# Score tiles from three 64-row products on two row groups instead of two stacked 128-row products

## The chip, the cores and the metric

The kernel runs on one core of a Trainium2 chip. Its engines are TensorE (PE in the profile; PEld is its weight load), VectorE (DVE), ScalarE (ACT), GpSimd (POOL) and SyncE (SP), which here only issues DMAs. The metric is the device time of one launch in microseconds (us): the median of the runs.

## The reference

For 8 batches with 8 heads of 576 rows and 64 columns, attention keeps the 32 largest scores of each row. Then each of the 4608 tokens goes to one of 8 experts with two layers.

```python
scores = scale * np.matmul(q, k.transpose(0, 1, 3, 2))
kth = np.partition(scores, -top_k, axis=-1)[..., -top_k:-top_k + 1]
scores = np.where(scores >= kth, scores, -1000000000.0)
attn = np.exp(scores - np.max(scores, axis=-1, keepdims=True))
attn = attn / (np.sum(attn, axis=-1, keepdims=True) + 1e-09)
x = np.matmul(attn, v)                  # per head; then [4608, 512]
logits = x @ w_gate + modality_bias[modality_id]
e_idx = np.argmax(logits, axis=1)       # gate_w: its softmax weight
h = np.maximum(x[mask] @ w1[e], 0.0)    # for each expert e
out[mask] = gate_w[mask, None] * (h @ w2[e])
```

## The kernel before, in words

Heads are worked in pairs: 32 pairs, each with nine tiles of 128 rows by 576 columns. Tiles 0 to 7 of a pair are four blocks of 128 rows for each of the two heads; the ninth holds the last 64 rows of both. A loop over steps i (L1056) records the work of all engines by hand, as a pipeline: at step i the scores of tile i + 2 are made, tile i is searched for its largest values on DVE, tile i - 9 is transposed, and the stages between run on ACT, POOL and DVE.

A score needs more precision than one pass of the fast type (fp32r) gives. So q and k are transposed on PE (prep, L280) and split into a high part and a remainder (split, L268), which lie in the tile st: two heads on partitions 0 to 63 and 64 to 127. Ten DMAs on SP's queue a pair (stack, L309) then copy them into stacked tiles. qs holds the high part of q on partitions 0 to 63 and the remainder on 64 to 127; ks holds the high part of k, or its remainder, on both halves. One product over 128 rows thus gives two terms, and two products all four. qk (L358) makes a tile in two halves of 288 columns, in two banks of PSUM, with two products each. For the ninth tile, fill (L322) copies the last 64 rows of q into two zeroed tiles qbd, one per head, and eight products of 512 or 64 columns make the tile. sevac (L375) copies a score tile from PSUM to SBUF on ACT; there is one PSUM buffer S for it.

The first pair takes no stacked tiles: unstacked (L341) makes two tiles at once, one per head, in S and T, from 64-row products out of st, four terms each.

The experts' work is cut into slots of 256 tokens. Once enough tokens are routed, a slot's matmuls (L775, L787) are recorded between the tiles. A planner decides how many: at each step it has a budget of STEP = 3.39, takes off what COST says the step's other PE work costs, and spends the rest (L1165 to L1178); where no slot is ready it records keep-warm matmuls (L913). The slots that are left at the end run alone, with products of three terms (L1005, L1021). avs and av (L491) multiply the attention weights with v, on two column groups.

Of the kernel before, what the change touches and what calls it, by code (L numbers as in the profile page):

```python
# [9 lines left out]
FT = mybir.dt.float32  # L10
# [43 lines left out]
COST = {"trans": 0.5, "qk": 0.5, "mix": 1.02, "rest": 0.22, "t": 0.11, "prep": 0.43, "logits": 1.2, "xrow": 0.54, "av": 0.49, "av8": 0.17}  # L54
# [18 lines left out]
def kernel(  # L73
# [40 lines left out]

    LD, PR, T = {}, {}, {}
# [57 lines left out]
    qbd = [[o.tile([128, 128], FR, name=f"qbd{i}{j}", bufs=1) for j in range(2)] for i, o in enumerate((const, wk))]  # L173
    for a in qbd:
        for t in a:
            V.memset(t.bitcast(FT), 0.0)
# [103 lines left out]
    def prep(p, part, first=False):  # L280
# [3 lines left out]
        if first:  # L284
            d.setdefault("st", st0)
        elif "st" not in d:
            d["st"] = wk.tile([128, 2, 2, S], FR, name="st", bufs=1)
# [16 lines left out]
        if part == "k":  # L304
            d["ks"] = wk.tile([128, 2, 2, S], FR, name="ks", bufs=2)
        else:
            d["qs"] = wk.tile([128, 2, S], FR, name="qs", bufs=2)

        def stack(h, queues=(SP, SP)):  # L309
            for v in range(2):  # L310
                if part == "k":
                    for a, b, o in ((0, S, 0),) if h == 0 else ((0, 512, 64), (512, S, -512)):
                        queues[v].dma_start(d["ks"][half(v), :, h, a + o:b + o].bitcast(FT), st[half(h), :, a:b].bitcast(FT))
                else:
                    queues[v].dma_start(d["qs"][half(v), h, :].bitcast(FT), st[half(h), v, :].bitcast(FT))

        for h in range(2):
            f = lambda h=h, **o: stack(h, **o)
# [14 lines left out]
    st0 = wk.tile([128, 2, 2, S], FR, name="ks", bufs=2)  # L333
    bd0 = wk.tile([128, 2, S], FR, name="qs", bufs=2)[:, 0, :256].rearrange("p (x s) -> p x s", x=2)

    def fill_first():
        for h in range(2):
            r = slice(h * 64, h * 64 + 64)
            G.tensor_scalar(bd0[r, :, r], PR[0]["st"][r, :, 1, 512:].bitcast(FT), 1.0, 1.0, op0=OP.mult, op1=OP.mult)

    def unstacked(j):  # L341

        if j % 2:
            return
        ps = [psS.tile([128, 2, 512], FT, name="S"), psT.tile([128, 2, 512], FT, name="T")][:1 + (j < 8)]
        for h, t in enumerate(ps):
            T[j + h] = {"ps": t[:, :, :288]}
        st = PR[0]["st"]
        r = [slice(h * 64, h * 64 + 64) if j < 8 else slice(0, 128) for h in range(2)]
        for x in range(2):  # L350
            for y in range(2):
                for h, a, b, o in ((0, 0, 288, 0), (1, 0, 64, 512), (1, 64, 288, -64), (0, 288, S, 0), (1, 288, S, -64)):
                    if h < len(ps):
                        l = bd0[:, x, :] if j == 8 else st[r[h], x, 1, j * 64:j * 64 + 128]
                        PE.matmul(ps[h][:, a // 288, a % 288:a % 288 + b - a], l, st[r[h], y, 0, a + o:b + o],
                                  start=(x + y == 0 and a % 288 == 0), stop=(x + y == 2), skip_group_check=True)

    def qk(i, p, j, bd):  # L358
        d = PR[p]
        ps = psS.tile([128, 2, 512], FT, name="S")  # L360
        for hf in range(2):
            a, b = (hf * 288, hf * 288 + 288) if j < 8 else ((0, 512), (512, S))[hf]
            if j < 8:
                c, h = divmod(j, 2)
                terms = [(d["qs"][:, h, c * 128:(c + 1) * 128], x, h, a, b, 0) for x in range(2)]
            else:
# [6 lines left out]
        T[i] = {"ps": ps[:, :, :288] if j < 8 else ps.rearrange("p a b -> p (a b)")[:, :S]}  # L373

    def sevac(i):  # L375
        T[i]["S"] = sb = wk.tile([128, S], FT, name="Ssb", bufs=LR + 1 + QL - QO)
        ps = T[i]["ps"]
        A.activation(sb.rearrange("p (a b) -> p a b", a=2) if len(ps.shape) == 3 else sb, ps, AF.Copy, scale=0.125)  # L378
# [536 lines left out]
    V.memset(bd0.bitcast(FT), 0.0)  # L915
# [21 lines left out]
    fill_first()  # L937
# [466 lines left out]
```

## Time and profile before

| | |
|---|---|
| median of 3 runs | 1266.87 us (1263.65 to 1268.3) |
| the profiled execution's own time | 1262.36 us |
| its span, first to last instruction | 1260.6 us |
| PE busy | 1181.1 us (94%) |
| PE's weight loads busy | 927.0 us (74%) |
| DVE busy | 1140.2 us (90%) |
| ACT busy | 989.0 us (78%) |
| POOL busy | 677.8 us (54%) |
| mean granted clock of PE | 0.986 |

Busy time is the union of the instructions' times on an engine. Matmuls overlap in the array, so that a matmul lasts longer than the distance to the next one: for throughput one reads the distances of starts. The granted clock is a share of 2.4 GHz: 1.00 is 2.4 GHz, 0.50 is 1.2 GHz.

### The profile page before, as it was taken

The numbers are of one execution on the slowest core, as the hardware profiler recorded it, in microseconds if no ns is written. First come the engines' busy times: TensorE is split into PE (matmuls) and PEld (weight loads), VectorE is DVE, ScalarE is ACT, GpSimd is POOL, SyncE is SP. The second block draws the span as 40 slices with busy tenths as digits, with TensorE's granted clock in tenths as the row PEclk, the third lists the DMA queues.
The fourth block names the chain that finished last, engine by engine and source line by source line (L and its number), as shares of the span: only waits on it lengthen the run. The fifth ranks groups of instructions, "written<-read, shape, count | busy, mean of one in ns | idle before, by whom it ended". The sixth has DMA issues, their size and how long they took to land. (4 is left out here: it accounts for less than half of the span.)

```text
span 1260.6 us, 28788 instructions
## 1 busy us (share of the span) xinstructions
PE 1181.1 (94%) x8032; PEld 927.0 (74%) x8032; DVE 1140.2 (90%) x5917; ACT 989.0 (78%) x2014; POOL 677.8 (54%) x1253
## 2 busy tenths in 40 slices
PE   7889987899988999989999999999999999999985
PEld 5667766768766868677777778787778775699885
DVE  6999999999999999999999999999999996477751
ACT  4999988889888988888898888888888885256542
POOL 4888865564574557554755466556755573211110
PEclk7999999999999999999999999999999999999998
DMA  4563337754356745655666566656576425478550
GB/s 107 156 186 86 87 86 224 199 150 126 86 136 188 217 117 157 189 156 139 171 184 177 146 182 191 185 154 169 161 207 178 128 71 168 150 251 275 190 174 15
DMA packets 204339, 199.28 MB, mean 158 GB/s; under 512 B 104413, under 2 KB 151533, under 8 KB 204160
## 3 DMA queue, kind: packets, MB, share of 16 engines
q1 hardware_dynamic: 196880, 177.96, 51.2%
q0 software_dynamic: 6080, 19.00, 4.2%
q8 instruction: 69, 1.13, 0.4%
q14 instruction: 110, 0.90, 0.2%
q10 hardware_dynamic: 1200, 0.30, 0.1%
HBM read 118.63 MB, written 24.23 MB: 113 GB/s over the span
## 5 line engine op out<-in xcount | busy, mean ns | idle before, releaser
L385 DVE MAX8 cand<-Ssb 128x8 f32<-128x82 f32 (+1 forms) x2016 | 429.5, 230 | 5.4 <-ACT Ssb L378 5.4
L423 POOL TENSOR_TENSOR y<-Ssb,K 128x576 f32<-128x576 f32 x288 | 370.4, 1286 | 5.7 <-ACT K L417 5.4
L417 ACT ACTIVATE K<-Ssb,n 128x576 bf16<-128x576 f32 x288 | 227.2, 789 | 29.0 <-POOL y L423 28.2
L378 ACT ACTIVATE Ssb<-S 128x576 f32<-128x576 f32 x284 | 185.9, 655 | 80.9 <-PE S L371 45.5
L371 PE MATMUL S<-ks,qs 128*128 128x288 f32 x992 | 220.3, 344 | 29.2 <-ACT Ssb L378 16.8
L427 DVE MAX8 mg<-y 128x8 f32<-128x576 f32 x288 | 214.7, 745 | 10.2 <-POOL y L423 10.2
L371 PEld LDWEIGHTS S<-ks,qs 128*128 128x128 f32 x992 | 151.5, 190 | 73.0 <-ACT Ssb L378 27.3
L775 PE MATMUL E<-xgT,w1b 128*128 128x256 f32 x816 | 196.8, 384 | 8.8 <-ACT hT L779 7.6
L441 ACT ACTIVATE ex<-Ssb,sm 128x576 f32<-128x576 f32 x256 | 199.9, 781 | 0.0
L489 ACT ACTIVATE PT<-T 128x640 f32<-128x640 f32 (+1 forms) x288 | 191.0, 663 | 5.6 <-PE T L481 5.6
L787 PE MATMUL E<-w2b,hT 128*128 128x512 f32 x400 | 188.2, 597 | 1.5 <-ACT hT L779 0.9
L447 DVE SCALAR_TENSOR_TENSOR P<-Ssb,kth,ex 128x576 f32<-128x576 f32 x224 | 188.0, 840 | 0.7 <-DVE cand L385 0.3
L481 PE MATMUL T<-idf,P 128*128 128x128 f32 x1152 | 170.4, 275 | 8.9 <-ACT P L466 8.9
L775 PEld LDWEIGHTS E<-xgT,w1b 128*128 128x128 f32 x816 | 147.5, 190 | 32.8 <-ACT hT L779 11.3
L470 POOL TENSOR_SCALAR spare<-P 1x1 f32<-1x1 f32 x224 | 50.0, 223 | 202.3 <-DVE mg L396 189.2
L481 PEld LDWEIGHTS T<-idf,P 128*128 128x128 f32 x1152 | 135.0, 140 | 17.9 <-ACT P L466 13.5
L509 PE MATMUL X<-PT,vm 128*64 128x256 f32 (+1 forms) x1536 | 145.0, 331 | 1.5 <-ACT xT L512 0.9
L410 POOL TENSOR_SCALAR n<-mg 128x1 f32<-128x1 f32 x288 | 72.8, 253 | 111.5 <-DVE mg L398 103.2
L509 PEld LDWEIGHTS X<-PT,vm 128*64 128x64 f32 x1536 | 88.4, 137 | 47.2 <-issue 10.2
L787 PEld LDWEIGHTS E<-w2b,hT 128*128 128x128 f32 x400 | 69.8, 190 | 59.7 <-issue 53.9
L1027 POOL DMA_INDIRECT out_dram<-ot,tk x12 | 12.0, 1000 | 106.7 <-ACT ot L1026 106.7
L396 DVE MAX8 mg<-cand 128x8 f32<-128x56 f32 x288 | 60.9, 211 | 0.2
(233 smaller groups left out, 2245.1 us busy)
## 6 DMA issues: line engine op xcount, KB each, us to landing
w1b<-in_moe_w_dram SPq DMA_DIRECT2D x76, 512.0 KB, 5.4
w2b<-in_moe_w_dram SPq DMA_DIRECT2D x76, 512.0 KB, 5.3
ks<-st SPq DMA_DIRECT2D x62, 288.0 KB, 3.4
qs<-st SPq DMA_DIRECT2D x124, 144.0 KB, 2.7
ks<-st SPq DMA_DIRECT2D x62, 256.0 KB, 4.8
xg<-xs SPq DMA_DIRECT2D x19, 516.0 KB, 5.1
km<-in_k_dram SPq DMA_DIRECT2D x64, 128.0 KB, 3.4
vm<-in_v_dram SPq DMA_DIRECT2D x32, 256.0 KB, 3.4
```

Source lines behind the costliest of these rows:

```text
L371: PE.matmul(ps[:, hf, u - a:v - a], l, d["ks"][:, x, h, u + o:v + o], start=(n == 0), stop=(n == len(terms) - 1), skip_group_check=(j == 8))
L385: return [lambda s=s: V.max(c[:, s * 8:s * 8 + 8], T[i]["S"][:, bnd[s]:bnd[s + 1]]) for s in range(NSUB)]
L417: A.activation(t["K"], t["S"], AF.Sign, scale=2.0 ** -24 - 1.0, bias=t["n"][:, 1, i % 3:i % 3 + 1], accum_out=t["n"][:, 0, i % 3:i % 3 + 1])
L423: G.tensor_tensor(t["y"], t["S"], t["K"], op=OP.mult)
L427: V.max(t["mg"][:, i % 3, 24:32], t["y"])
L441: A.activation(t["ex"], t["S"], AF.Exp, bias=t["s"][:, i % 3:i % 3 + 1])
L447: V.scalar_tensor_tensor(t["P"], t["S"], kth[:, i:i + 1], t["ex"], op0=OP.is_ge, op1=OP.mult, accum_out=dn)
L481: PE.transpose(T[i]["pt"][:, x, :], (Pm if c == 4 else Pb[c % 2])[:, h * 512 + x * 128:h * 512 + x * 128 + 128], idf)
L489: A.activation(o, T[i]["pt"][:, :n], AF.Copy)
L509: PE.matmul(o.rearrange("p (a b) -> p a b", a=2) if j < 8 else o, l, r, start=(c == 0), stop=(c == 4))
L775: PE.matmul(ps[:, f % 2], w1b[:, c, f * 128:(f + 1) * 128], xgT[:, c, :], start=(c == 0), stop=(c == KC - 1))
L787: PE.matmul(o["py"], hT[:, f, t * 128:(t + 1) * 128], w2b[:, f, :], start=(f == 0), stop=(f == FC - 1))
```

## The change

qk now makes each of tiles 0 to 7 from three terms (high by high, high by remainder, remainder by high) in two halves of 288 columns. A product has 64 rows. The half with g = 0 takes its operands from partitions 0 to 63, the other from 64 to 127; for the head that lies on the right partitions they come from st itself, for the other half from sw, into which cross copies each head's q and part of its k onto the other head's partitions: five DMAs a pair. st has two buffers now. The ninth tile takes six products of 128 rows and 288 columns from one zeroed tile that holds both heads' rows on its diagonal. The first pair drops the fourth term. The planner's costs of a score tile go from 0.5 to 0.4 and, for the ninth, from 1.02 to 0.8.

```diff
-COST = {"trans": 0.5, "qk": 0.5, "mix": 1.02, ...
+COST = {"trans": 0.5, "qk": 0.4, "mix": 0.8, ...
+    TERMS = ((0, 0), (0, 1), (1, 0))
-            d["st"] = wk.tile([128, 2, 2, S], FR, name="st", bufs=1)
+            d["st"] = wk.tile([128, 2, 2, S], FR, name="st", bufs=2)
...
+            d["sw"] = wk.tile([128, 2, 512 + 288], FR, name="sw", bufs=2)
+        def cross(h):
+            if part == "q":
+                cols = ((0, 512, 0),)
+            else:
+                cols = ((288, S, 512),) if h == 0 else ((512, S, 512), (0, 224, 576))
+            for a, b, o in cols:
+                SP.dma_start(d["sw"][half(1 - h), :, o:o + b - a].bitcast(FT), st[half(h), :, a:b].bitcast(FT))
...
     def fill(p, bd):
         for h in range(2):
-            G.tensor_scalar(bd[h][:, h * 64:h * 64 + 64], PR[p]["qs"][:, h, 512:].bitcast(FT), 1.0, 1.0,
-                            op0=OP.mult, op1=OP.mult)
+            r = slice(h * 64, h * 64 + 64)
+            G.tensor_scalar(bd[r, :, r], PR[p]["st"][r, :, 1, 512:].bitcast(FT), 1.0, 1.0, op0=OP.mult, op1=OP.mult)
...
     def unstacked(j):
-        for x in range(2):
-            for y in range(2):
+        for x, y in TERMS:
...
     def qk(i, p, j, bd):
-        for hf in range(2):
-            a, b = (hf * 288, hf * 288 + 288) if j < 8 else ((0, 512), (512, S))[hf]
-            if j < 8:
-                c, h = divmod(j, 2)
-                terms = [(d["qs"][:, h, c * 128:(c + 1) * 128], x, h, a, b, 0) for x in range(2)]
-            else:
-                terms = [(bd[0], x, 0, a, b, 0) for x in range(2)]
-                for u, v, o in ((a, min(b, 512), 64), (512, b, -512)):
-                    terms += [(bd[1], x, 1, u, v, o) for x in range(2)] if u < v else []
-            for n, (l, x, h, u, v, o) in enumerate(terms):
-                PE.matmul(ps[:, hf, u - a:v - a], l, d["ks"][:, x, h, u + o:v + o], start=(n == 0),
-                          stop=(n == len(terms) - 1), skip_group_check=(j == 8))
+        c, h = divmod(j, 2)
+        for x, y in TERMS:
+            for g in range(2):
+                r = slice(g * 64, g * 64 + 64)
+                if j == 8:
+                    l, m = bd[:, x, :], st[:, y, 0, g * 288:g * 288 + 288]
+                elif g == h:
+                    l, m = st[r, x, 1, c * 128:c * 128 + 128], st[r, y, 0, h * 224:h * 224 + 288]
+                else:
+                    l, m = d["sw"][r, x, c * 128:c * 128 + 128], d["sw"][r, y, 512:]
+                PE.matmul(ps[:, g, :288], l, m, start=(x + y == 0), stop=(x == 1), skip_group_check=True)
```

On PE, at a ninth tile and the tile behind it, in the stage in which expert work runs between the tiles, the program before has these rows (S is the score tile, T the transposes' tile, E the experts'; P and idf are transposed values and the identity):

```order
L775 MATMUL E<-xgT,w1b 128x256 x4
L371 MATMUL S<-ks,qbd_117 128x512 x2
L371 MATMUL S<-ks,qbd_118 128x512 x2
L371 MATMUL S<-ks,qbd_117 128x64 x2
L371 MATMUL S<-ks,qbd_118 128x64 x2
L481 MATMUL T<-idf,P_124 128x128 x4
L775 MATMUL E<-xgT,w1b 128x256 x6
L371 MATMUL S<-ks,qs 128x288 x4
L481 MATMUL T<-idf,P_124 128x128 x5
```

On PE in the changed program, at such a place, L762 and L774 are the experts' lines, L360 is qk's and L468 the transposes':

```order
L762 MATMUL E<-xgT,w1b 128x256 x6
L360 MATMUL S<-st,qbd_116 128x288 x6
L468 MATMUL T<-idf,P_120 128x128 x4
L774 MATMUL E<-w2b,hT 128x512 x3
L360 MATMUL S<-st 128x288
L360 MATMUL S<-sw 128x288
L360 MATMUL S<-st 128x288
L360 MATMUL S<-sw 128x288
L360 MATMUL S<-st 128x288
L360 MATMUL S<-sw 128x288
L468 MATMUL T<-idf,P_120 128x128 x5
```

The ninth tile has six equal products where it had eight of two widths. An ordinary tile has six products that alternate between st and sw, and so between the two halves of the partitions, where it had four; expert matmuls still stand ahead of it and transposes behind it.

On SP's queue, the copies of one pair before:

```order
L313 DMA ks<-st 64x2x576 x2
L313 DMA ks<-st 64x2x512
L313 DMA ks<-st 64x2x64
L313 DMA ks<-st 64x2x512
L313 DMA ks<-st 64x2x64
L315 DMA qs<-st 64x576 x4
```

The copies of one pair on SP's queue in the changed program:

```order
L312 DMA sw<-st 64x2x288
L312 DMA sw<-st 64x2x64
L312 DMA sw<-st 64x2x224
L312 DMA sw<-st 64x2x512 x2
```

Ten transfers became five, at the same places of the queue.

## Rows read from the trace of the kernel before

**Rows 1.** Busy time by stretch: start:end, length, each engine's busy (instructions), PEclk, DMA.

```profile
8.00:25.00 17.00, 15.62 (x88) 12.75 (x86) 11.88 (x81) 7.17 (x15) 9.21 (x19) 0.50 0.33 80
40.00:280.00 240.00, 210.74 (x1640) 165.86 (x1638) 237.99 (x1324) 214.37 (x468) 170.31 (x266) 1.00 0.55 146
280.00:560.00 280.00, 264.94 (x1833) 205.73 (x1831) 274.30 (x1505) 240.61 (x496) 159.96 (x305) 0.99 0.55 152
560.00:1040.00 480.00, 473.08 (x3153) 364.89 (x3151) 469.30 (x2552) 413.21 (x850) 289.69 (x553) 1.00 0.60 164
1080.00:1230.00 150.00, 145.99 (x897) 126.86 (x896) 97.69 (x262) 75.91 (x117) 21.05 (x48) 1.00 0.64 215
```

**Rows 2.** Waits, 560 to 1040 us: engine line <- releaser: us in total, times, longest.

```profile
ACT Ssb L378 <- PE S L371: 27.0, 29, 1.8
```

**Rows 3.** Timeline of PE, 700 to 708 us: start, length of the group, instructions.

```profile
699.62 1.67 PE L775 MATMUL E<-xgT,w1b 128*128 128x256 f32 x7
700.95 1.64 PE L371 MATMUL S<-ks,qbd 128*128 128x512 f32 x8
702.42 0.65 PE L481 MATMUL T<-idf,P 128*128 128x128 f32 x4
702.91 2.76 PE L775 MATMUL E<-xgT,w1b 128*128 128x256 f32 x12
705.32 0.88 PE L371 MATMUL S<-ks,qs 128*128 128x288 f32 x4
706.03 0.71 PE L481 MATMUL T<-idf,P 128*128 128x128 f32 x5
```

**Rows 4.** Timeline of PE in the startup, 12.7 to 13.2 us.

```profile
12.78 0.44 PE L355 MATMUL S<-ks 64*128 64x288 f32 x1
12.79 0.53 PE L355 MATMUL T<-ks 64*128 64x224 f32 x1
13.02 0.44 PE L355 MATMUL S<-ks 64*128 64x288 f32 x1
13.12 0.47 PE L355 MATMUL T<-ks 64*128 64x288 f32 x1
```

**Rows 5.** Timeline of PE around products on two column groups, 314.3 to 318.4 us.

```profile
314.35 0.27 PE L290 MATMUL X<-idf,kqt 128*128 128x128 f32 x1
314.55 1.95 PE L509 MATMUL X<-PT,vm 128*64 128x256 f32 x16
...
316.76 0.63 PE L509 MATMUL X<-PT,vm 128*64 128x64 f32 x16
317.22 0.29 PE L509 MATMUL X<-PT,vt 128*64 128x64 f32 x4
317.44 0.80 PE L371 MATMUL S<-ks,qs 128*128 128x288 f32 x4
318.08 0.49 PE L481 MATMUL T<-idf,P 128*128 128x128 f32 x3
```

**Rows 6.** Timeline of PE and its loads at the first pair; [idle before <- releaser].

```profile
14.85 0.18 PEld L290 LDWEIGHTS X<-idf,kqt 128*128 128x128 f32 x1 [0.25 <-issue]
...
21.52 1.05 PE L297 MATMUL X<-idf,qm 128*128 128x128 f32 x4
22.51 0.28 PEld L355 LDWEIGHTS S<-ks 64*128 64x128 f32 x1 [0.33 <-issue]
...
22.51 0.61 PE L355 MATMUL S<-ks 64*128 64x288 f32 x1
22.92 0.44 PE L355 MATMUL S<-ks 64*128 64x288 f32 x1
```

**Rows 7.** Waits, 40 to 1040 us.

```profile
PE S L371 <- DMA qs<-st: 8.3, 5, 2.9
```

**Rows 8.** All instructions of L371: count, ns min/median/max, first and last start.

```profile
L371 PE MATMUL S<-ks,qs x992: 289/296/702, 31.9 to 1030.0; 128*128 128x288 f32 x199
L371 PE MATMUL S<-ks,qbd x248: 191/332/802, 54.2 to 1033.7; 128*128 128x512 f32 x62, 128*128 128x64 f32 x62
```

More of the change, by code (lines that the diff above doesn't have):

```diff
@@ L53 @@
 AV7 = (0, 5)
-COST = {"trans": 0.5, "qk": 0.5, "mix": 1.02, "rest": 0.22, "t": 0.11, "prep": 0.43, "logits": 1.2, "xrow": 0.54, "av": 0.49, "av8": 0.17}
+COST = {"trans": 0.5, "qk": 0.4, "mix": 0.8, "rest": 0.22, "t": 0.11, "prep": 0.43, "logits": 1.2, "xrow": 0.54, "av": 0.49, "av8": 0.17}
 RN = 6
@@ L171 @@
     G.iota(tokc[:, 4:5], pattern=[[1, 1]], base=512, channel_multiplier=1, allow_small_or_imprecise_dtypes=True)
[L173 to L176, printed above, removed]
+    qbd = [o.tile([128, 2, 128], FR, name=f"qbd{i}", bufs=1) for i, o in enumerate((const, wk))]
+    for t in qbd:
+        V.memset(t.bitcast(FT), 0.0)
     Pb = [wk.tile([128, 2 * S], FT, name=f"P{i}", bufs=1) for i in range(2)]
@@ L283, in prep @@
         d = PR.setdefault(p, {})
-        if first:
-            d.setdefault("st", st0)
-        elif "st" not in d:
-            d["st"] = wk.tile([128, 2, 2, S], FR, name="st", bufs=1)
+        if "st" not in d:
+            d["st"] = wk.tile([128, 2, 2, S], FR, name="st", bufs=2)
         if part == "t":
@@ L304, in prep @@
         if part == "k":
-            d["ks"] = wk.tile([128, 2, 2, S], FR, name="ks", bufs=2)
-        else:
[L307 to L315, printed above, removed]
+            d["sw"] = wk.tile([128, 2, 512 + 288], FR, name="sw", bufs=2)
[6 more added lines that the diff above has]
+                SP.dma_start(d["sw"][half(1 - h), :, o:o + b - a].bitcast(FT), st[half(h), :, a:b].bitcast(FT))
         for h in range(2):
-            f = lambda h=h, **o: stack(h, **o)
+            f = lambda h=h: cross(h)
             f.move = True
@@ L331, in flush @@
             x.clear()
[L333 to L339, printed above, removed]
     def unstacked(j):
@@ L344, in unstacked @@
             return
-        ps = [psS.tile([128, 2, 512], FT, name="S"), psT.tile([128, 2, 512], FT, name="T")][:1 + (j < 8)]
+        ps = [psS.tile([128, 2, 512], FT, name="S"), psT.tile([128, 2, 512], FT, name="T")]
+        st = PR[0]["st"]
         for h, t in enumerate(ps):
             T[j + h] = {"ps": t[:, :, :288]}
-        st = PR[0]["st"]
-        r = [slice(h * 64, h * 64 + 64) if j < 8 else slice(0, 128) for h in range(2)]
-        for x in range(2):
-            for y in range(2):
[L352 to L356, printed above, removed]
+        for x, y in TERMS:
+            for h, a, b, o in ((0, 0, 288, 0), (1, 0, 64, 512), (1, 64, 288, -64), (0, 288, S, 0), (1, 288, S, -64)):
+                r = slice(h * 64, h * 64 + 64)
+                PE.matmul(ps[h][:, a // 288, a % 288:a % 288 + b - a], st[r, x, 1, j * 64:j * 64 + 128],
+                          st[r, y, 0, a + o:b + o], start=(x + y == 0 and a % 288 == 0), stop=(x == 1),
+                          skip_group_check=True)
@@ L358, in qk @@
     def qk(i, p, j, bd):
         d = PR[p]
+        st = d["st"]
         ps = psS.tile([128, 2, 512], FT, name="S")
[L361 to L372 removed]
@@ L375, in sevac @@
+        T[i] = {"ps": ps[:, :, :288]}
     def sevac(i):
         T[i]["S"] = sb = wk.tile([128, S], FT, name="Ssb", bufs=LR + 1 + QL - QO)
-        ps = T[i]["ps"]
-        A.activation(sb.rearrange("p (a b) -> p a b", a=2) if len(ps.shape) == 3 else sb, ps, AF.Copy, scale=0.125)
+        A.activation(sb.rearrange("p (a b) -> p a b", a=2), T[i]["ps"], AF.Copy, scale=0.125)
     bnd = [(x * S) // NSUB for x in range(NSUB + 1)]
@@ L936 @@
         prep(0, part, True)
-    fill_first()
+    fill(0, qbd[0])
     modality = bias_loads()
@@ L1069, in scores @@
                 pp, jj = divmod(i + QL, 9)
-                if pp == 0:
+                if pp == 0 and jj < 8:
                     unstacked(jj)
```

3 lines of the change are left out of this document (removed).

## The prediction

> **What bounds the kernel now.** I read four views, in this order. First the busy time by stretch [rows 1]. From 560 to 1040 us TensorE (PE) is busy 473.08 of 480 us and VectorE (DVE) 469.30; from 1080 to 1230 us, with attention over, PE is busy 145.99 of 150 us and DVE only 97.69. The reader is to see two stages: one in which PE and DVE are both full, and a tail in which PE alone is. Before 280 us PE idles 29.3 of 240 us, between 280 and 560 us 15.1 us, and in 560 to 1040 us only 6.9 us. DVE idles 2.0 + 5.7 + 10.7 = 18.4 us between 40 and 1040 us: that is all that attention can give back, since a tile can't be faster than its work on DVE.
>
> Second the waits [rows 2]. From 560 to 1040 us ScalarE waits 29 times, 27.0 us in all, for the score matmuls of L371: PE is late with score tiles. So time taken from PE there, or added to it, can show in the end.
>
> The program's order says what fills PE. The work of the experts is recorded between the tiles by a planner with a budget of 3.39 us a tile. Both programs hold 448 matmuls of the experts' first layer and 224 of the second ahead of the part with three products (13 slots, and one in the fallback that runs only on bad thresholds), and 418 keep-warm matmuls. The lower costs of the new plan move expert work some tiles ahead, and no further slot into attention: the tail keeps its 6 slots.
>
> **The score tile before.** At 2.4 GHz (granted clock 1.00) the rows of L775 follow each other every (2.76 - 1.67)/(12 - 7) = 0.218 us, so twelve that start at 702.91 us are through the array at 705.52. The four score matmuls behind them are followed by the first transpose at 706.03 [rows 3]: 0.51 to 0.53 us a tile, 0.13 us a matmul, with the weight loads hidden. The ninth tile of a pair starts behind seven L775 (699.62 + 7 x 0.218 = 701.15) and its transpose starts at 702.42 [rows 3]: 1.28 us for its eight matmuls.
>
> **What the change does to it.** Two terms in two halves become three terms in two halves. If the halves run on both row groups at once, a tile streams 3 x 288 columns in place of 4 x 288: 0.13 us less. The startup shows that they do: the first pair's products are 64-row ones already. At granted clock 0.50 (1.2 GHz) [rows 1] S starts every 0.24 us (12.78, 13.02), which is 288 columns at that clock, while T's products run beside them (12.79, 13.12) [rows 4].
>
> But each tile now goes from the full array to two row groups and back, since the expert matmuls ahead of it and the transposes behind it are 128-row ones. What such a change of shape costs is in the trace. At 2.4 GHz it is seen where the attention-times-values matmuls of L509 (two column groups) begin and end [rows 5]. The transpose of L290 starts at 314.35 and takes a spacing of 0.11 us, as the five transposes in [rows 3] do ((0.71 - 0.27)/4), so the array is free at 314.46; L509 starts at 314.55: 0.09 us of nothing. At the end, the 64-column products run at (317.22 - 316.76)/8 = 0.058 us a pair, so the last two pairs are through at 317.34; L371 starts at 317.44: 0.10 us. And its four matmuls then take 318.08 - 317.44 = 0.64 us and not 0.53, since no weights could be loaded ahead: 0.11 us. For the two row groups themselves the trace has only the 1.2 GHz side. The matrix loads idle 0.33 us before the first L355 at 22.51, against none between loads in the same shape; the first product is 0.41 us ahead of the second where the others are 0.24 apart: 0.17 us; and on the way out the load of L290 at 14.85 waits 0.25 us for nothing that the profile shows [rows 6]. (The Trainium skill, "TensorEngine Tiling", section "Key Properties", says that changing the tiling mode, not just the tile, drains TensorE. The rows agree; without a drain a tile would be 0.13 us cheaper, with one it is dearer.)
>
> So a tile of the new kind costs: drain in 0.09, first load 0.11, three pairs 3 x 0.13 = 0.39, drain out 0.10, first load of the transposes 0.11, together 0.80 us against 0.53: **0.27 us more**. The lower bound halves what the 1.2 GHz rows lose: of the 0.33 us some 0.2 are the stream of the last transpose (its row has four in 1.05 us), so drain in 0.07; load 0.17/2 = 0.08; of the 0.25 us some 0.1 are the end of the last product, so drain out 0.08; load 0.08; with 0.39 that is 0.70: 0.17 more. The other end is a shape change at no cost, 0.13 us less. I take 0.27, from the rows at the clock at which nearly all tiles run.
>
> The ninth tile stays on the full array: 6 x 0.13 = 0.79 us against 1.28, **0.49 us less**. A pair of heads: 8 x 0.27 - 0.49 = **+1.67 us of PE** (bounds +0.9 and -1.5).
>
> **What else moves.** Ten stacking transfers a pair become five, with under half the bytes. PE waited for them in 5 places from 40 to 1040 us, 8.3 us in all [rows 7]; where PE has become the later engine, such a wait is time to catch up, so I count nothing beside the idle time below. POOL's two copies for the ninth tile move half the partitions each; POOL idles and nothing waits for them. The second buffer of st only loosens a wait. The first pair loses one of four terms: two S spacings of 0.24 us [rows 4] on the path to DVE's first tile, about -0.5 us.
>
> **The sum.** Pairs take (1033.7 - 31.9)/31 = 32.3 us, from the first start of the eight-tile form and the last of the ninth tiles' [rows 8]. From 560 us to the last scores there are 14.7 of them: 14.7 x 1.67 = +24.5 us on an engine that never catches up again, for the tail is PE's too. It can absorb what it idles there, 6.9 us, of which I take half, since some of that is waiting for ScalarE: -3.5. From 280 to 560 us 8.7 pairs add 14.5 us where 15.1 us are idle: nothing left. Before that, idle time covers it. With the startup: 24.5 - 3.5 - 0.5 = +20.5 us. Against the profiled execution's own 1262.36 us that is 1282.9; it lies 4.5 us under the median of the runs, 1266.87, from which it would be 1287.4. I say **1285 us**. With the lower bound (+0.9 a pair) it is 13.2 - 3.5 - 0.5 = +9, so 1272 to 1276; with nothing absorbed after 280 us, 23.4 x 1.67 = +39, so 1301 to 1306. The likeliest case's own range is 1272 to 1305.
>
> **Rivals.** *The row groups pay off (faster).* Its place is the border between score tile and neighbours: if the array takes 64-row products without draining, a pair costs 8 x (-0.13) - 0.49 = -1.5 us. It decides where a border costs under (0.13 + 0.49/8)/2 = 0.10 us each way; the rows give 0.2. For it speaks that S and T do run together [rows 4]. The gain would stop at DVE: at most its 18.4 us, by half about -9, and some -4 us for expert work that gets out of the way of the tail by the new plan, so 1250, at best 1244. (The Trainium skill's "TensorEngine Tiling", section "Theoretical Speedup", gives up to 2x for a contraction of 64 or less: by it this rival holds. The rows show the twofold streaming and the price of the border beside it.)
>
> *The borders cost, and slack takes it (no change).* ScalarE copies the scores two tiles ahead of their use, which is some 7 us of play. If expert matmuls wait in PE's place and DVE never starves, and the price is at the lower bound, the end moves by 0 to 6 us: 1262 to 1273. Against it: PE is full up to the end of the tail, so its added work has nowhere to go.
>
> *The lag starves DVE in expert-rich tiles and idles PE in poor ones (slower still).* The new plan packs expert work earlier and leaves three poor tiles in each batch of 36. For it speaks that both engines are full, so that a tile lost on PE isn't won back by DVE. If PE idles 4 us, a poor tile's worth, in each of the four batches after 560 us, 16 us come on top: 1301. Against it: by then PE is late by more than that, and works the poor tiles off without idling.
>
> **How the numbers follow.** A measurement can tell about 0.5% (6.3 us) from no change. The forecast has 0.62, still slower 0.09, no change 0.14, faster 0.15. Faster by over 0.5% (under 1260.5): 0.15; within: 0.13; slower (over 1273.2): 0.72. The range for 8 in 10 goes from 1257, which leaves out most of the faster rival, to 1305.
>
> **What would show it.** In the profile after, the six products of a tile should start in pairs a few ns apart, the pairs 0.13 us apart once running; ahead of the first pair and ahead of the next transposes PE should show about 0.1 us without a start, and the first spacing should be 0.24 us. From 560 us to the end of attention PE should stay full and DVE's idle time grow by 15 us or more; attention should end near 1060 us, and the stretch from there to the end keep its length within 5 us. If tiles follow their neighbours with no gap, the forecast is wrong at its price; if the gaps are there and the time is not, it is wrong in calling PE the bound.

## The result: slower by 9.5 us, under half of the forecast

The changed kernel takes 1274.35 us (median of 6, 1272.36 to 1276.89), the kernel before 1264.87 us beside it (6 runs): ratio 1.0071, 95% interval 1.0053 to 1.0088. The direction was forecast, and the border between tile shapes as its reason; the size was not, with +20.5 us. The profiled execution has a span of 1270.7 us and a time of 1272.36 us.

Busy time by stretch in the changed kernel, columns as in [rows 1]:

```profile
8.00:25.00 17.00, 13.24 (x79) 10.23 (x78) 14.58 (x100) 10.93 (x23) 11.18 (x22) 0.70 0.41 97
280.00:560.00 280.00, 269.21 (x1942) 188.78 (x1937) 273.43 (x1504) 238.38 (x488) 159.75 (x307) 0.99 0.44 126
560.00:1040.00 480.00, 475.88 (x3290) 327.92 (x3290) 465.44 (x2473) 407.32 (x831) 278.33 (x537) 1.00 0.46 134
1080.00:1230.00 150.00, 147.65 (x926) 126.19 (x922) 101.13 (x278) 74.20 (x117) 22.23 (x46) 1.00 0.64 213
```

From 560 to 1040 us PE is busier than before (475.88 against 473.08) and DVE does less in the same time (465.44 against 469.30): attention runs slower there, and PE sets it. The waits of that stretch, against [rows 2]:

```profile
ACT Ssb L365 <- PE S L360: 41.9, 53, 1.6
...
DVE x L530 <- PE X L529: 11.2, 8, 3.2
```

ScalarE waits 53 times for score tiles where it waited 29 times, and VectorE now waits for the transposed rows that the router needs.

The timeline of PE at one ordinary tile and one ninth tile, against [rows 3]:

```profile
691.46 2.75 PE L762 MATMUL E<-xgT,w1b 128*128 128x256 f32 x12
694.14 0.40 PE L360 MATMUL S<-sw 64*128 64x288 f32 x1
694.14 0.40 PE L360 MATMUL S<-st 64*128 64x288 f32 x1
694.38 0.29 PE L360 MATMUL S<-sw 64*128 64x288 f32 x1
694.38 0.29 PE L360 MATMUL S<-st 64*128 64x288 f32 x1
694.51 0.29 PE L360 MATMUL S<-sw 64*128 64x288 f32 x1
694.52 0.29 PE L360 MATMUL S<-st 64*128 64x288 f32 x1
694.74 0.76 PE L468 MATMUL T<-idf,P 128*128 128x128 f32 x5
...
703.58 1.89 PE L762 MATMUL E<-xgT,w1b 128*128 128x256 f32 x8
705.12 1.14 PE L360 MATMUL S<-st,qbd 128*128 128x288 f32 x6
706.10 0.60 PE L468 MATMUL T<-idf,P 128*128 128x128 f32 x4
```

The halves start together, as forecast. The expert matmuls start 0.216 us apart (median of 391 spacings; the prediction's 0.218, from two rounded rows, is a little long), so twelve leave the array free at 691.46 + 12 x 0.216 = 694.05. It idles 0.09 us, the first pair takes 0.24 us (0.11 more than the others), the array is free again at 694.65 and idles 0.09 us before the transposes; their row of five lasts 0.76 us where it lasted 0.71, another 0.05. So this tile takes 694.74 - 694.05 + 0.05 = 0.74 us against 0.53: **+0.21 us**, not the +0.27 of the forecast. It is typical: the median of 80 such tiles from 280 to 1040 us is +0.21 as well. The ninth tile: 703.58 + 8 x 0.216 = 705.31 to 706.10, 0.79 us against 1.28, -0.49 as forecast.

About one ordinary tile in ten stands behind products on two column groups and not behind expert products. There the kernel before already pays to come back to the full array [rows 5], and the change costs only 0.01 us (medians of 11 and 7 tiles, 560 to 1040 us). So the average is lower, and one batch (36 tiles, four pairs) gives it. The rows show the stretch between the starts of the 181st and the 217th search of the rank (MAX8 of mg from y); columns as above. Before, then after:

```profile
665.63:797.50 131.87, 130.69 (x873) 100.88 (x872) 129.24 (x704) 114.80 (x237) 79.56 (x153) 1.00 0.62 171
```

```profile
664.91:801.04 136.13, 134.80 (x929) 92.87 (x927) 131.60 (x705) 115.76 (x236) 78.35 (x153) 1.00 0.48 138
```

PE does 4.11 us more in a batch, 1.03 a pair, and with -0.50 for each ninth tile that is **+0.19 us** for the average ordinary tile. The batch is 4.26 us longer. Before, PE idled only 1.2 us in a batch.

When that is paid shows in the first and last start of this search (count, ns min/median/max, first to last start). Before, then after:

```profile
L427 DVE MAX8 mg<-y x288: 729/744/762, 23.0 to 1054.3; 128x8 f32<-128x576 f32 x144
```

```profile
L414 DVE MAX8 mg<-y x288: 730/745/764, 19.7 to 1065.5; 128x8 f32<-128x576 f32 x144
```

The changed kernel starts 3.3 us ahead and ends attention 11.2 us behind. It keeps its lead up to the 145th tile (2.4 us ahead, at 533 us) and loses 13.6 us in the four batches after that. From the last search to the end it needs 205.2 us, before 206.3.

### The profile page after: what moved, and what is told of

It reads as the page before. It is cut to its first block, busy times and chain, and to the rows that moved or that the text cites. A ratio compares the mean times of both kernels' runs of the same rounds, so it can differ in the third digit from the quotient of the medians.

```text
span 1270.7 us, 29267 instructions
## 1 busy us (share of the span) xinstructions
PE 1200.8 (94%) x8444; PEld 866.6 (68%) x8444; DVE 1150.2 (91%) x5914; ACT 994.5 (78%) x2014; POOL 676.0 (53%) x1253
## 5 line engine op out<-in xcount | busy, mean ns | idle before, releaser
L410 POOL TENSOR_TENSOR y<-Ssb,K 128x576 f32<-128x576 f32 x288 | 367.6, 1276 | 12.4 <-ACT K L404 11.8
L762 PE MATMUL E<-xgT,w1b 128*128 128x256 f32 x832 | 201.4, 384 | 4.7 <-ACT xgT L733 2.6
L434 DVE SCALAR_TENSOR_TENSOR P<-Ssb,kth,ex 128x576 f32<-128x576 f32 x224 | 196.6, 878 | 0.7 <-DVE cand L372 0.3
L468 PE MATMUL T<-idf,P 128*128 128x128 f32 x1152 | 181.4, 285 | 12.4 <-ACT P L453 11.3
L774 PE MATMUL E<-w2b,hT 128*128 128x512 f32 x400 | 185.5, 595 | 0.7 <-ACT hT L766 0.7
L360 PE MATMUL S<-st 64*128 64x288 f32 x744 | 164.5, 327 | 15.7 <-ACT Ssb L365 14.8
L762 PEld LDWEIGHTS E<-xgT,w1b 128*128 128x128 f32 x832 | 149.9, 190 | 29.4 <-ACT xgT L733 4.1
L360 PE MATMUL S<-sw 64*128 64x288 f32 x744 | 163.4, 326 | 5.8 <-ACT Ssb L365 3.1
L468 PEld LDWEIGHTS T<-idf,P 128*128 128x128 f32 x1152 | 124.5, 141 | 53.9 <-issue 27.8
L360 PEld LDWEIGHTS S<-st 64*128 64x128 f32 x744 | 106.2, 185 | 68.6 <-ACT Ssb L365 24.0
L457 POOL TENSOR_SCALAR spare<-P 1x1 f32<-1x1 f32 x224 | 43.2, 193 | 199.5 <-DVE mg L383 181.2
L496 PE MATMUL X<-PT,vm 128*64 128x256 f32 (+1 forms) x1536 | 148.0, 336 | 1.3 <-ACT xT L499 0.8
L360 PEld LDWEIGHTS S<-sw 64*128 64x128 f32 x744 | 106.1, 185 | 47.0 <-issue 11.8
L774 PEld LDWEIGHTS E<-w2b,hT 128*128 128x128 f32 x400 | 70.4, 190 | 61.5 <-issue 59.2
```

Source lines behind the costliest of these rows:

```text
L360: PE.matmul(ps[:, g, :288], l, m, start=(x + y == 0), stop=(x == 1), skip_group_check=True)
L410: G.tensor_tensor(t["y"], t["S"], t["K"], op=OP.mult)
L434: V.scalar_tensor_tensor(t["P"], t["S"], kth[:, i:i + 1], t["ex"], op0=OP.is_ge, op1=OP.mult, accum_out=dn)
L468: PE.transpose(T[i]["pt"][:, x, :], (Pm if c == 4 else Pb[c % 2])[:, h * 512 + x * 128:h * 512 + x * 128 + 128], idf)
L496: PE.matmul(o.rearrange("p (a b) -> p a b", a=2) if j < 8 else o, l, r, start=(c == 0), stop=(c == 4))
L762: PE.matmul(ps[:, f % 2], w1b[:, c, f * 128:(f + 1) * 128], xgT[:, c, :], start=(c == 0), stop=(c == KC - 1))
```

## The experiments

The kernel before was run beside each group (its medians: 1264.42, 1264.55, 1266.63 and 1264.68 us). Ratios are against it, with their 95% intervals.

### The plan and the border apart

**The ninth tile alone**, with the new cost for it:

```
... (buffers moved to make room; "mix" 1.02 to 0.8 in COST)
+ for x, y in ((0, 0), (0, 1), (1, 0)) if j == 8 else ():   # six products, unstacked q and k
+     for g in range(2): PE.matmul(ps[:, g, :288], bd[:, x, :], d["K"][:, y, g * 288:...], ...)
- if j == 3 and 0 < p < NPAIR: fill(p, ...)
+ if j == 3 and p + 1 < NPAIR: fill(p + 1, ...)
```

> The kernel before with the ninth tile alone changed (six full-array products of 288 columns, planned at 0.8); the stacked products of tiles 0 to 7 and their copies stay. Border theory (score tiles lose by the change of the array's shape, ninth tiles gain 0.49 us each): PE loses 0.49 us a pair, 7 us over the 14.7 pairs after 560 us, and DVE lets about half through: 3 to 7 us faster than before, 1258 to 1262 us. Planner theory (the loss comes from expert work that is recorded earlier): within 2 us of before or slower. DVE theory (the loss is DVE's longer select-and-multiply of L434, 196.6 us in all after the change against 188.0): the time follows that sum, whatever PE does.

1275.65 us, 1.0094 (1.0076 to 1.0113), 11.2 us slower, which only the planner theory allows. But the trace shows another cause. GpSimd's second copy into the block-diagonal tile waits once in a batch, and with it GpSimd's product y, which VectorE's search reads:

```profile
768.35 0.29 POOL L325 TENSOR_SCALAR qbd<-st 64x128 fp32r<-64x128 f32 x1
770.85 0.29 POOL L325 TENSOR_SCALAR qbd<-st 64x128 fp32r<-64x128 f32 x1 [2.21 <-issue]
```

The waits of that search from 560 to 1060 us; in the kernel before they are 7.6 us, the longest 0.6:

```profile
DVE mg L432 <- POOL y L428: 13.5, 15, 2.8
```

From 40 us on VectorE waits 20.1 us for y, before 10.0; those 10 us are nearly as large as the loss. Why the copy waits is open, and the new cost of the ninth tile and the earlier copy weren't run apart, so that the planner theory is only made unlikely for this run.

**The change with the old costs**, and **the kernel before with the new costs**:

```
- COST = {"trans": 0.5, "qk": 0.4, "mix": 0.8, ...}
+ COST = {"trans": 0.5, "qk": 0.5, "mix": 1.02, ...}     # and the reverse in the kernel before
```

> The changed kernel with the planner's old costs (0.5 and 1.02), so that expert work is recorded where it was. Border theory: as the changed kernel within 4 us, 1270 to 1278 us, since the score tiles' shape changes stay. Planner theory: back to the kernel before within 3 us, 1262 to 1268 us. DVE theory: back only if the sum of DVE's select-and-multiply falls from 196.6 to near 188.

1267.47 us, 1.0025 (1.0010 to 1.0040).

> The kernel before with the planner's new costs (0.4 and 0.8) and nothing else. Border theory: as the kernel before within 3 us, 1262 to 1268 us. Planner theory: 6 us slower or more, 1271 us and up. DVE theory: slower by as much as the sum of the select-and-multiply (188.0 us before) grows.

1281.14 us, 1.0131 (1.0109 to 1.0153). So the cost table, which the prediction counted at nothing, costs 16.7 us under the old score product and 1274.35 - 1267.47 = 6.9 us under the new one. The same batch with the old costs under the change (first), and with the new costs in the kernel before (second):

```profile
661.68:796.17 134.49, 134.49 (x933) 93.00 (x929) 129.63 (x704) 116.25 (x238) 79.48 (x153) 1.00 0.49 140
```

```profile
670.87:810.22 139.35, 133.88 (x873) 103.21 (x871) 132.25 (x704) 114.65 (x237) 76.86 (x153) 0.98 0.60 162
```

With the old costs PE works through the whole batch of the changed kernel. With the new ones it idles 1.3 us of a batch under the change and 5.5 us in the kernel before. The new plan packs the expert work closer: in this batch of the kernel before it leaves three score tiles in a row with no expert matmul ahead of them, and under the change four, where the old plan leaves only single ones. VectorE waits for what PE does behind the packed stretch, and in the poor tiles PE runs dry. In the changed kernel the longest such wait, [idle before <- releaser], falls on the router's rows:

```profile
696.41 0.69 DVE L530 TENSOR_TENSOR x<-X,rd 128x512 f32<-128x512 f32 x1 [3.20 <-PE X L529]
```

From one search to the next it makes that tile 7.22 us long, against 5.05 with the old costs and 4.04 before.

Where PE runs dry in the kernel before with the new costs, it waits for transfers, the stacked copies above all. Its waits for them from 560 to 1040 us:

```profile
PE S L371 <- DMA kqt<-in_k_dram: 8.2, 2, 4.4
PE S L371 <- DMA qs<-st: 4.8, 3, 3.5
```

Once in a batch PE reaches a score tile 3.5 to 4.4 us before the transfer has landed. From 40 to 1060 us it waits 21.2 us at score tiles for transfers, with the old costs 8.3, and under the change, with either table, 2.0. The 12.9 us between the first two are most of the size of the 16.7, and more than the difference between 16.7 and 6.9. Whether the change avoids these waits by its five copies or by the second buffer of st wasn't separated.

**The border by itself**, in the kernel before: ahead of each ordinary tile's four products two products of 16 columns on the two row groups.

```
+ for g in range(2 if j < 8 else 0):
+     r = slice(g * 64, g * 64 + 64)
+     PE.matmul(ps[:, g, :16], d["qs"][r, 0, :128], d["ks"][r, 0, 0, :16], start=True, stop=True, ...)
```

> The kernel before with two more products of 64 rows and 16 columns, one on each row group, ahead of the four of each ordinary tile; the four overwrite what they leave. It adds two borders a tile and next to no stream. Border theory, with the prices of the changed kernel's trace: drain in 0.09, load 0.10, stream 0.03, drain out 0.10, load 0.11, so 0.43 us a tile and 3.4 us a pair; over the 23.4 pairs after 280 us 80 us, less some 15 to 25 us of idle time: 55 to 70 us slower than before, 1320 to 1335 us. Theory without a border price: 0.03 us a tile, 0 to 5 us slower.

1317.03 us, 1.0419 (1.0394 to 1.0444), 52.6 us more. Timeline of PE, and the batch:

```profile
705.95 2.76 PE L778 MATMUL E<-xgT,w1b 128*128 128x256 f32 x12
708.64 0.28 PE L363 MATMUL S<-ks,qs 64*128 64x16 f32 x2
708.85 0.79 PE L374 MATMUL S<-ks,qs 128*128 128x288 f32 x4
709.47 0.27 PE L484 MATMUL T<-idf,P 128*128 128x128 f32 x1
```

```profile
688.79:831.51 142.72, 142.72 (x941) 105.73 (x942) 132.25 (x705) 115.95 (x238) 79.80 (x153) 1.00 0.58 160
```

Array free at 705.95 + 12 x 0.216 = 708.54; 0.10 us to the short pair, 0.21 to the first full product, and 0.62 instead of 0.53 from there to the transposes: 0.40 us for a way out of the full array and back. The batch agrees: PE does 142.72 - 130.69 = 12.03 us more on 32 tiles; five other matmuls that fall into this stretch are some 0.6 of it, and 0.36 a tile is left, with the cheaper tiles behind column groups in it. The change's own borders come to 0.74 - 3 x 0.13 = 0.35 us at a tile behind expert products. A shape change that costs nothing, the condition of the fast rival, is refuted.

### The start

```
- for h, a, b, o in (... five products ...):
+ for h, a, b, o in () if x + y == 2 else (... five products ...):
```

> The kernel before with one edit: the first pair's score tiles lose their fourth term (low part of q by low part of k), as the change has it; the score product, the plan's costs and all else stay. In the trace the change starts its first rank search on VectorE 3.3 us earlier than the kernel before. Theory A, the shorter first pair itself (10 of the 40 products of each two tiles are gone, at half the clock): 2 to 3 us faster, 1262 us. Rival B, the fewer startup transfers of the change: this edit moves no transfer, so no change within 1 us. Rival C, the start is hidden behind the inputs' landing, as the prediction had it: 0.5 us faster.

1263.33 us, 0.9989 (0.9975 to 1.0002): 1.2 us between the medians, and the first search starts at 21.8 us instead of 23.0. The time alone, -3.2 to +0.3 us, doesn't tell A from the rivals. Nor can the starts of two single executions be compared: the granted clock from 8 to 25 us was 0.50 in the trace before and 1.00 in this one. But the border run (four terms at the start) and the changed kernel with the scatters moved (reported below; three terms and five copies) were caught at 1.00 too. Border run, three terms, changed kernel:

```profile
L430 DVE MAX8 mg<-y x288: 729/746/764, 23.7 to 1108.3; 128x8 f32<-128x576 f32 x144
L427 DVE MAX8 mg<-y x288: 729/746/766, 21.8 to 1052.9; 128x8 f32<-128x576 f32 x144
L414 DVE MAX8 mg<-y x288: 730/745/761, 21.8 to 1069.6; 128x8 f32<-128x576 f32 x144
```

In these three executions that is 1.9 us for the dropped term, near A's size, and nothing for the fewer transfers. Over all profiled runs the first search of kernels with four terms lies at 22.0 to 23.7 us (seven runs, mean 23.1), with the change's start at 19.7 to 21.9 (eight, mean 20.9): the 3.3 us between the two traces above are 2.2 on average.

### A collision on VectorE, and what it is worth

In the changed kernel VectorE's masked product (SCALAR_TENSOR_TENSOR, usually 0.80 us) takes up to 1.92 us when GpSimd's product y runs at the same time. VectorE, then GpSimd:

```profile
618.92 1.92 DVE L434 SCALAR_TENSOR_TENSOR P<-Ssb,kth,ex 128x576 f32<-128x576 f32 x1
```

```profile
618.95 1.26 POOL L410 TENSOR_TENSOR y<-Ssb,K 128x576 f32<-128x576 f32 x1
```

y is late there behind a row scatter (xs, 1.02 us of GpSimd's queue, five in a batch). All such products together, before and after (xcount | busy us, mean ns):

```profile
L447 DVE SCALAR_TENSOR_TENSOR P<-Ssb,kth,ex 128x576 f32<-128x576 f32 x224 | 188.0, 840 | 0.7 <-DVE cand L385 0.3 <-ACT Ssb L378 0.2
```

```profile
L434 DVE SCALAR_TENSOR_TENSOR P<-Ssb,kth,ex 128x576 f32<-128x576 f32 x224 | 196.6, 878 | 0.7 <-DVE cand L372 0.3 <-ACT ex L428 0.2
```

8.6 us more: a second theory for the plan's 6.9 us. The first edit against it moved the scatter behind y:

```
+ if sends and seen[0]: sends.popleft()()     # now between pool_y(i - LY) and below(i - 1)
```

> The changed kernel with one edit: GpSimd's row scatter (xs, 1.02 us of its queue, five in a batch) is issued behind the product y instead of at the end of the step before it. In the trace of the changed kernel y comes late behind these scatters, starts while VectorE's masked product (P from the scores) runs or just before it, and the masked product then lasts 1.2 to 1.9 us instead of 0.80: 16.0 us in all, against 8.1 us in the kernel before. Theory A, the new plan costs what it costs because these two collide: most of the 16 us go from VectorE, and the time falls by 6 to 10 us, to 1264 to 1268. Rival B, the plan costs because TensorE comes late with the score tiles after each rich stretch, and the collisions are only a sign of it: the collisions go, VectorE waits for scores instead, and the time falls by 3 us at most. Rival C, the scatter now holds up GpSimd's small operation that ScalarE's sign pass waits for: slower than 1274.

> The kernel before with the same edit as the run beside it: the row scatter behind the product y. Here the collisions take 8.1 us of VectorE, one of 0.46 us in most batches at the first scatter. Theory A, collisions cost what they add to VectorE: 2 to 4 us faster, 1261 to 1263 us, less than the changed kernel gains by the same edit. Rival B: within 1 us of before, since VectorE's lead is given back at the score tiles. Rival C, the held-up small operation: slower by 2 us or more.

> The changed kernel with the old cost table (which alone gave 1267.5 us) and the row scatter behind the product y. Theory A, what is left of the change's cost under the old plan is the border time of TensorE, and the collisions are as in the kernel before: it falls by as much as the kernel before does by the same edit, 2 to 4 us, to 1264 or 1265. Rival B, part of the 3 us that the change costs under the old plan is collisions too: it falls further, to 1261 or 1262, level with the kernel before with this edit.

1274.85 us, 1.0080 (1.0066 to 1.0093); 1266.21 us, 1.0008 (0.9997 to 1.0020); 1271.32 us, 1.0048 (1.0033 to 1.0062). The edit missed: it reached only the first batch's five scatters, which don't collide; the later ones are issued from the list of small steps. The collisions stayed (16 us of excess in the changed kernel), so no theory is tested. Why the third lost 3.9 us against the change with the old costs is open (2.9 by the ratios, whose intervals overlap); it warns that two programs that differ in five places of one queue can lie that far apart.

The second edit moves the scatters of all batches but the last:

```
- side.extend(store + [done])
+ side.extend([(lambda f=f: held.append(f)) if b1 < B - 1 and ... else f for x, f in enumerate(store)] + [done])
+ while held: held.popleft()()                # between pool_y(i - LY) and below(i - 1)
```

> The changed kernel with the row scatters of all batches but the last issued behind the product y on GpSimd. The run that meant to do this moved only the first batch's five scatters, which do not collide; the later batches issue theirs through another list. Theory A, the new plan costs time through the collisions of y with VectorE's masked product: the excess of the masked product over 0.82 us falls from 16 to under 8 us and the time from 1274.4 to 1264 to 1268. Rival B, TensorE's late score tiles are the cost and the collisions their sign: the excess falls all the same, VectorE waits for score tiles instead, and the time stays above 1271. Rival C, the scatter holds up the small operation behind it, which ScalarE's sign pass waits for: slower than 1274.

> The kernel before with the same edit, all batches but the last. Theory A: the 0.46 us at the first scatter of most batches and the 2.6 us of the third batch go, together some 5 us of VectorE: 2 to 5 us faster, 1260 to 1262, less than the changed kernel gains. Rival B: within 1.5 us of before. Rival C: slower by 2 us or more.

> The changed kernel with the old cost table and the scatters moved in all batches but the last. The old cost table alone gave 1267.5 us, and its excess of the masked product is 8.3 us, as in the kernel before. Theory A, the border time is what is left: it falls as far as the kernel before with the same edit, 2 to 5 us, to 1263 to 1265, and stays 2 to 4 us behind that kernel. Rival B, what is left is collisions: level with the kernel before with the same edit, within 1.5 us.

> The kernel before with the first pair's three terms (1.2 us faster by itself) and the scatters moved in all batches but the last: a candidate to be faster than both kernels. If the two gains add: 1.2 plus 2 to 5, 1258 to 1261 us. If the scatters gain nothing (rival B of the run beside it): 1263.

The changed kernel: 1275.76 us, 1.0076 (1.0057 to 1.0095). The kernel before: 1257.66 us, 0.9937 (0.9917 to 0.9956). The change with old costs: 1268.48 us, 1.0023 (1.0010 to 1.0036). The kernel before with three terms: 1254.11 us, 0.9904 (0.9883 to 0.9925).

In the changed kernel the masked products fall to 189.4 us, and the time doesn't: the collisions were a sign, not the plan's cost, and my second theory falls. In the kernel before the same edit gains 8 to 9 us, where I expected 5 at most, and with the three terms it passes the 1258 expected. The collisions are the smaller part of what it frees there. The masked products fall from 188.0 to 184.2 us:

```profile
L447 DVE SCALAR_TENSOR_TENSOR P<-Ssb,kth,ex 128x576 f32<-128x576 f32 x224 | 184.2, 822 | 0.7 <-issue 0.5
```

VectorE's waits for y, which no longer stands behind a scatter in GpSimd's queue, fall from 10.2 us to 0.2 (| busy us, mean ns | idle before); the kernel before, then with the scatters moved:

```profile
L427 DVE MAX8 mg<-y 128x8 f32<-128x576 f32 x288 | 214.7, 745 | 10.2 <-POOL y L423 10.2
L427 DVE MAX8 mg<-y 128x8 f32<-128x576 f32 x288 | 214.5, 745 | 0.2 <-POOL y L423 0.2
```

How much of the 8 to 9 us each of the two gave wasn't separated. The run with the ninth tile alone speaks for the waits: there they grow by 10 us while the masked products stay (188.9 us), and the time grew by 11.

The batch of the kernel before with the scatters moved, then of the change with old costs and the scatters moved:

```profile
658.89:789.86 130.97, 130.73 (x875) 100.92 (x873) 129.17 (x705) 114.21 (x237) 77.00 (x153) 1.00 0.63 173
```

```profile
660.77:796.86 136.09, 136.09 (x945) 94.09 (x946) 131.71 (x704) 117.62 (x241) 77.93 (x153) 1.00 0.48 138
```

With y out of the way the kernel before runs at PE's own 130.7 us a batch, and the changed kernel has no idle PE to win back. (Its stretch holds 16 matmuls of attention times values more than the others, so its length isn't to be compared.) With the old costs the edit took away its waits for y too, from 10.2 us to 0.5, though not its collisions (masked products 188.5 and 189.1 us), and its time didn't fall. So VectorE's losses around y had hidden a part of the change's cost: with the scatters moved and old costs in both, the change is 10.8 us behind (1268.48 against 1257.66).

### The ninth tile once more, and true costs

The ninth tile with old costs and the copy four steps later (`if j == 7 and ...: fill(p + 1, ...)`), alone and on top of the fastest kernel so far:

> The kernel before with only the ninth tile in the change's form (six products of 288 columns, the split q and k read unstacked), the old costs, and GpSimd's copy into the block-diagonal tile four steps later than in the first such run, where its second half held GpSimd up by 2.2 us once in a batch. Theory A, before this edit TensorE has 1.3 us of a batch to spare, because VectorE loses more than that in collisions: 0.5 us less per ninth tile buys nothing, within 2 us of before. Rival B, TensorE sets the pace and each ninth tile counts: 14 or 15 pairs by 0.5 us, 7 us faster, 1258. Rival C, this form of the ninth tile costs something itself, as the first run (1275.7 us) suggests: 5 us or more slower.

> The same ninth tile together with the moved scatters and the first pair's three terms, which without it gave 1254.1 us. With the scatters moved TensorE is idle 0.2 us in a batch of 131 us, so now each ninth tile should count. Theory A, TensorE sets the pace once the collisions are gone: 0.5 us by four pairs is 2 us in each of some 4 batches, less what VectorE can't follow (it is idle 1.8 us in a batch), 1247 to 1251 us. Rival B, VectorE sets it: within 2 us of 1254.

1265.17 us, 1.0005 (0.9992 to 1.0018), and **1249.28 us, 0.9874 (0.9851 to 0.9896)**, the fastest of all, ahead of both kernels. Alone the six products leave PE idle 3.0 us of a batch where it idled 1.2, and buy no time; where PE sets the pace they are worth 4 to 5 us (0.9904 to 0.9874; 1254.11 to 1249.28). The intervals of these two ratios overlap, but the batches agree: 131.00 us without the new ninth tile, 129.77 with it. The batch of the ninth tile alone, then of all three edits:

```profile
667.13:799.26 132.13, 129.18 (x866) 99.67 (x865) 130.07 (x704) 114.57 (x238) 78.99 (x153) 1.00 0.62 169
659.95:789.72 129.77, 129.11 (x868) 99.76 (x866) 129.01 (x705) 114.48 (x239) 76.95 (x153) 1.00 0.64 173
```

The comparison isn't clean: in the run alone the moved copy made new collisions (masked products 193.0 us against 188.0) and took away some waits for y (6.7 us against 10.0 from 40 us on), so VectorE lost about as much as before by another way.

Last, the changed kernel with its borders in the costs, without and with the scatters moved:

```
- COST = {"trans": 0.5, "qk": 0.4, "mix": 0.8, ...}
+ COST = {"trans": 0.5, "qk": 0.73, "mix": 0.8, ...}
```

> The changed kernel with the cost of an ordinary score tile at 0.73 (0.53 us of products and 0.21 us of borders, as its trace shows) in place of 0.4, the ninth at 0.8 as the change has it. Theory A, the change's plan loses some 7 us because its costs leave out the borders, so that it hands out too much expert work at a time, and the rows that the router needs come through TensorE's queue 2 us later once in a batch: right costs give 1266 to 1269 us, as the old table did (1267.5). Rival B, any plan that hands out less work per step leaves expert work for the tail, at TensorE's pace: 1274 or slower. Rival C, the plan doesn't matter by size but by where single waits happen to fall: anything from 1264 to 1280, with no relation to the costs.

> The same costs with the scatters moved. Under the old costs and under the change's own the moved scatters gained the changed kernel nothing (1268.5 against 1267.5, 1275.8 against 1274.4), though they gained the kernel before 8 us. Theory A, the changed kernel is bound by TensorE, so the scatters gain nothing here either: within 2 us of the run beside it. Rival B, what hid the gain was the crowded plan: 4 us or more faster than the run beside it.

1274.01 us, 1.0068 (1.0048 to 1.0088), and 1273.83 us, 1.0070 (1.0048 to 1.0092). Rival B comes out (C's wide range can't be excluded by the time alone): attention now ends 17.7 us ahead of the changed kernel, and one expert slot more is left for the tail, seven by 24 products of each term instead of six:

```profile
L414 DVE MAX8 mg<-y x288: 729/744/762, 21.8 to 1047.8; 128x8 f32<-128x576 f32 x144
```

```profile
L990 PE MATMUL X<-xgh,w1h 128*128 128x256 f32 x168 | 48.1, 287 | 3.2 <-ACTq L1283 3.2
```

The same row of the changed kernel:

```profile
L990 PE MATMUL X<-xgh,w1h 128*128 128x256 f32 x144 | 41.8, 290 | 3.7 <-DVEq L1283 3.7
```

The tail grows from 205.2 to 226.0 us. The long wait at the router's rows is gone (that tile takes 3.92 us and not 7.22), so true costs do what theory A says to attention; but PE's work has to be done in one place or the other. The scatters again gain the changed kernel nothing.

## Why the prediction was wrong

| step | forecast | measured |
|---|---|---|
| ordinary tile | +0.27 us | +0.21 behind expert products, +0.19 on average (batch: 4.11 = 32 x 0.19 - 4 x 0.50) |
| ninth tile | -0.49 | -0.50 |
| pair of heads | +1.67 | +1.03 |
| pairs from 560 us | 14.7: +24.5 | +15.1 |
| idle PE that absorbs, 560 to 1040 us | -3.5 | -2.8 (6.9 us idle before, 4.1 after) |
| startup | -0.5 | -3.3 at the first search of these two traces |
| sum | +20.5 | +9.0; the traces' spans say +10.1, the medians +9.5 |

**The step that failed is the border price of the ordinary tile.** The prediction had the right parts, two drains and two exposed loads, but summed them at 0.41 us ("drain in 0.09, first load 0.11, ... drain out 0.10, first load of the transposes 0.11"); they measure 0.09 + 0.11 + 0.09 + 0.05 = 0.34 at a tile behind expert products. Three of the four were right; the last load was not. It was taken from a 288-column score product behind the column-group products, 0.64 against 0.53, and what follows a score tile are transposes, whose first spacing shows 0.05. The other part of the error is the tiles that stand behind column groups, one in ten, which the prediction charged like the rest. Together 0.08 us a tile, by eight tiles and 14.7 pairs 9.4 us. The prediction's own lower bound (+0.17 a tile, +0.9 a pair, 1272 to 1276 us) met the result, but by halving what rows at 1.2 GHz lose, with each load at 0.08: its sum is right and its parts are not.

**The startup was undersized,** too: the prediction gave the dropped term two spacings of S, 0.5 us. In executions at the same clock it shows 1.9, and the two traces of the table happen to lie 3.3 apart.

**The plan was not free, and by luck that brought the number nearer.** The prediction let the costs "move expert work some tiles ahead" and gave that no term; they cost 6.9 us. Without them the change is at +3 us, and the forecast would have been some 17 us too high, not 11. There PE idles 0.5 us from 560 to 1040 us, so nearly all its idle time is taken, which by the table's terms makes 15.1 - 6.4 - 2.8 = +5.9. The two traces' spans are 5.0 us apart (1265.6 and 1260.6); the way from there to +3 is that the trace before is of a quick execution, 2.1 us under the median beside this run. The 0.9 us left are not explained.

**The bound was named right, with one thing missed.** PE does set the pace of the changed kernel, and the tail kept its length within 5 us, as forecast. But in the kernel before part of PE's idle time was made by VectorE's losses around y, collisions and waits, in rows that I didn't look at. The forecast sign that VectorE's idle time would grow by 15 us or more from 560 us to the end of attention did not come: up to the last search it grew from 11.0 to 15.0 us only, while its busy time grew by 7.2 us, with the longer masked products in it. Of the rivals, the fast one falls with the border runs; the slack took 2.8 us of 15; the one in which the lag starves VectorE named a right mechanism, a wait of 3.2 us once in a batch. Its other half, 4 us of idle PE in a batch, which I had argued against, is absent in the changed kernel (1.3 us) and there in the kernel before with the new costs (5.5 us, of which 4.4 is one wait for a transfer).

## What to carry to other kernels

Price a change of the array's shape from rows with the same kind of instruction on both sides of the border: the drains were alike at both kinds of border (0.09 to 0.10 us), the exposed load was not (0.11 and 0.05). A planner's cost table is a change of its own; run the new code with the old table and the old code with the new one before crediting the code. Where two engines are both nearly full, ask what makes the idle time of the second: here a saving on PE that bought nothing alone went with 4 to 5 us once VectorE's losses around y were gone.

## What the runs showed of the hardware that was not expected

VectorE's product of two inputs and GpSimd's product of two inputs hold each other up, and which of them waits depends on a tenth of a microsecond. In the changed kernel GpSimd's y starts 0.03 us after VectorE's product, keeps its 1.26 us, and VectorE's lasts 1.92 instead of 0.80. In the kernel before, at 620.31, VectorE's starts 0.16 us ahead of y and keeps its 0.82 us, and y lasts 1.80 instead of 1.27. It is no single case: in the two traces y keeps its time in all five collisions in which it starts 0.03 or 0.04 us after VectorE's product, and VectorE's product keeps its time in all six in which y starts 0.16 to 0.18 us after it:

```profile
620.31 0.82 DVE L447 SCALAR_TENSOR_TENSOR P<-Ssb,kth,ex 128x576 f32<-128x576 f32 x1
```

```profile
620.47 1.80 POOL L423 TENSOR_TENSOR y<-Ssb,K 128x576 f32<-128x576 f32 x1
```

The Trainium skill, "SBUF — State Buffer", section "SBUF: two separate sides", says that a VectorE operation with two inputs in SBUF and a GpSimd operation that reads SBUF lock a shared port pair against each other for the whole instruction, and that the one that starts first has it. The trace agrees on the lock: the loser ends 0.63 us (VectorE) or 1.14 us (GpSimd) after the winner. By the starts that the profile shows, the later one won at 618.95; as the profile's times on GpSimd are rough, it isn't shown that it truly began later.
